# The state update of a linear attention head by head, in two column halves of the TensorE array

## The chip, the cores and the metric

The kernel runs on one core of one Trainium2 chip. The metric is the device time of one execution in microseconds (us), from the first to the last instruction and the little that lies around them. An engine is named as in the profile: PE is TensorE (PEld its weight loads), DVE VectorE, ACT ScalarE, POOL GpSimd, SP the queue that issues most transfers.

## What is computed

A linear attention with a decaying state, then two feed-forward networks on its output. Batch 4, 8 heads, 768 time steps, head size 48:

```python
for t in range(S):
    kt, vt, rt, wt = (k[:, :, t], v[:, :, t], r[:, :, t], w[:, :, t])
    cur = np.einsum('bhd,bhe->bhde', u[None] * kt, vt)
    y[:, :, t] = np.einsum('bhd,bhde->bhe', rt, state + cur)
    state = wt[:, :, :, None] * state + np.einsum('bhd,bhe->bhde', kt, vt)
...
h = x @ w_in
g = h * np.clip(h + 3.0, 0.0, 6.0) / 6.0
x = g @ w_out
...
h = x @ w_in2
solu = h * softmax(h)
out = (layernorm(solu) * g_ln) @ w_out2
```

The change concerns the last line of the time loop: the sum over time of the outer products of k and v, one 48x48 state for each head and batch.

## The kernel before

The sequence is cut into 6 blocks (`g`) of 128 steps. With 4 batches that makes 24 tiles `i = 4 g + b`, each of 8 heads. Five stages handle a tile: `stw` clamps and range-checks w, `st0` transposes w and r to the layout head size x time (PE, into PSUM) and forms running products of w (DVE scans, L484 and L490), `st1` does k, `st2` forms the masked products of r and k (`pa`, L543, `am`, L550 to L554) and the decayed k with time on the partitions (`ktok`, L534), and `st3` makes the state update `kv` (L563) and the output `yt` (L578, L585).

Heads go in pairs: two heads of 48 lie at partitions 0 to 47 and 64 to 111 (`DP = 112`). In `st3`, for tiles of all blocks but the last (20 tiles), `kv` is four matmuls, one for a pair of heads: `ktok` of the pair (112 columns) are the weights, `v` of both heads (96 columns) streams through, both with 128 time steps on the partitions, all in float32. Of the 112x96 result only the two 48x48 blocks on the diagonal are wanted. L604 (DVE, from block 1 on) and L606 (ACT, block 0) take them out of PSUM into the state `s_st`.

`yt` works in column quarters of the array (32 or 16 weight columns at output partition 0, 32, 64 or 96), `pa` in row halves (48 rows at partition 0 or 64).

The feed-forward work is threaded between the attention's stages: for each block 16 slots, each with `ffn_in` (9 matmuls 128x512, L635) and `ffn_out` (9, L655), with ACT L639 and L641, DVE L640 and POOL or DVE L643 between them. At the start the first network's weights are also decoded, chunk by chunk: `raw` (loads L353 to L358) goes through DVE L40, L43, ACT L44, DVE L50, L53, then ACT L60 (`w_h`) and DVE L61 (`w_l`). After block 5 the second network runs (L828 to L858).

The attention's PSUM tiles `wt`, `rt`, `kt`, `ktp`, `pa0`, `pa1`, `kv`, `yt` share one pool of three buffers (`ps_a`, L339, L434). A fourth tile can only be written once the last reader of the first is done.

Every engine runs its instructions in the order in which they stand. For PE, DVE and ACT a scheduler sets that order from what it thinks an instruction costs; the loads on SP and the work on POOL are written out by hand for the first ticks (L739 and what follows) and scheduled after that. So a change of one group's form can move other instructions as well.

Of the kernel before, what the change touches and what calls it, by code (L numbers as in the profile page):

```python
# [267 lines left out]
def fast_path(  # L268
# [15 lines left out]
    B, H, S, D = r.shape  # L284
# [5 lines left out]
    HP = H // 2  # L290
    DP = 112
# [38 lines left out]
        out=causal.bitcast(F32), in_=ones, pattern=[[1, P]], compare_op=ALU.is_gt, fill=0.0, base=0,  # L330
# [102 lines left out]
    def ps_tile(nm):  # L433
        return ps_a.tile([P, 4, P], F32, tag="pa", name=nm)  # L434
# [121 lines left out]
    def st3(i):  # L556
        a = at[i]
        g, b = divmod(i, B)
        if g < NG - 1:
            vv = a["v"].rearrange("p h d -> p (h d)")  # L560
            kv = ps_tile("kv")
            for hp in range(HP):
                nc.tensor.matmul(  # L563
                    out=kv[0:DP, hp, 0:2 * D], lhsT=a["ktok"][:, hp, :], rhs=vv[:, hp * 2 * D:(hp + 1) * 2 * D],
                    start=True, stop=True,
                )
        y = ps_tile("yt")

        def inter(c, first):
            for q in range(4):  # L570
                if c < 2:
                    h = 4 * c + q
                    hp, f = h // 2, D * (h % 2)
                    lhs = a["sp"][0:DP, hp, f:f + 32]
                else:
                    hp = q
                    lhs = a["sr"][0:DP, q, :]
                nc.tensor.matmul(  # L578
                    out=y[32 * q:32 * q + 32, c, :], lhsT=lhs, rhs=a["e"][0:DP, hp, :], start=first, stop=not first,
                    skip_group_check=True,  # L580
                )

        def intra(c, heads, lo, n, first, last):
            for q, h in enumerate(heads):
                nc.tensor.matmul(  # L585
                    out=y[32 * q:32 * q + n, c, :], lhsT=a["v"][:, h, lo:lo + n], rhs=a["am"][h % 2][:, h // 2, :],
                    start=first, stop=last, skip_group_check=True,
                )

        for c in range(2):  # L590
            if g > 0:
                inter(c, True)
            intra(c, range(4 * c, 4 * c + 4), 0, 32, g == 0, True)
        intra(2, range(1, H, 2), 16, 32, True, False)
        intra(2, range(0, H, 2), 32, 16, True, g == 0)
        if g > 0:
            inter(2, False)
        if g < NG - 1:
            for j in range(2):
                o, f = 64 * j, D * j  # L600
                dst = s_st[b][o:o + D, :, f:f + D]
                src = kv[o:o + D, :, f:f + D]
                if g > 0:
                    nc.vector.tensor_tensor(out=dst, in0=src, in1=a["sp"][o:o + D, :, f:f + D], op=ALU.add)  # L604
                else:
                    nc.scalar.activation(out=dst, in_=src, func=ACTF.Copy)  # L606
        at.pop(i)
        if b == 0:
            x_t[g] = (
                xp.tile([P, KD, GT], F32R, tag="xh", name="xh"),  # L610
                xp.tile([P, KD, GT], F32R, tag="xl", name="xl"),
            )
        xh, xl = x_t[g]
        sl = slice(b * C, (b + 1) * C)
        xf = y[:, 0:KD, :]
        nc.scalar.activation(out=xh[:, :, sl], in_=xf, func=ACTF.Copy, accum_out=chk[:, 3 * i + 2:3 * i + 3])
        nc.vector.tensor_tensor(out=xl[:, :, sl], in0=xf, in1=xh[:, :, sl].bitcast(F32), op=ALU.subtract)
# [301 lines left out]
```

## Time and profile before

| | |
|---|---|
| time, median of 3 runs | 795.32 us (794.71 to 795.42) |
| the profiled execution's own time | 796.49 us |
| its span, first to last instruction | 794.8 us |
| mean granted clock of TensorE in it, 1 is 2.4 GHz | 0.978 |
| PE busy | 753.4 us (95%) |
| PEld busy | 634.3 us (80%) |
| DVE busy | 543.2 us (68%) |
| ACT busy | 331.9 us (42%) |
| POOL busy | 272.9 us (34%) |

The profile names an instruction by line, engine, operation and tiles. A matmul row gives weight rows * weight columns and then partitions x streamed columns (`128*112 128x96`). One float32 matmul is two records: L563 has 160 for 80 matmuls. Matmuls are pipelined: the length of one record holds its way through the array, so what a matmul costs a full PE is read from the distance between starts, not from its length.

### The profile page before, as it was taken

What the parts mean: (1) busy time and instruction counts of PE and PEld (TensorE: products, weight loads), DVE (VectorE), ACT (ScalarE), POOL (GpSimd) and SP (SyncE); (2) the same over time, 40 slices, a digit from 0 to 9 for tenths busy, and PEclk for the clock granted to TensorE, in tenths of its full rate; (3) what the DMA queues carried; (4) which work ended last, traced back from release to release, by engine and by line L of the source; (5) the groups of instructions that cost most, each with busy time, mean ns of one, the idle gap of its engine ahead of it and who ended that gap; (6) DMA issues with size and microseconds to landing.
All of it is one profiled execution on the core that took longest, in us unless ns stands there. A gap on an engine that the chain in (4) does not pass through costs nothing. (4 is left out here: it accounts for less than half of the span.)

```text
span 794.8 us, 13227 instructions
## 1 busy us (share of the span) xinstructions
PE 753.4 (95%) x4922; PEld 634.3 (80%) x4922; DVE 543.2 (68%) x1038; ACT 331.9 (42%) x615; POOL 272.9 (34%) x355
## 2 busy tenths in 40 slices
PE   5689898899999999999999999999999999999996
PEld 4567676688888888888888888777889999999996
DVE  5989799856777777777777675895365555555552
ACT  3354544342334433444434334544343443443342
POOL 5487545647333333333232212231122222222210
PEclk9889799999999999999999999999999999999999
DMA  9777455235333433343323212430111111111001
GB/s 167 175 155 162 118 132 138 51 93 124 79 83 91 114 83 84 75 122 81 73 64 93 53 50 61 131 119 1 52 49 40 41 41 51 40 43 48 30 21 35
DMA packets 139432, 64.75 MB, mean 81 GB/s; under 512 B 90848, under 2 KB 133984, under 8 KB 139360
## 3 DMA queue, kind: packets, MB, share of 16 engines
q1 hardware_dynamic: 136768, 59.11, 31.2%
q10 hardware_dynamic: 2592, 4.72, 1.6%
q8 instruction: 41, 0.67, 0.4%
q14 instruction: 31, 0.25, 0.1%
HBM read 54.37 MB, written 9.44 MB: 80 GB/s over the span
## 5 line engine op out<-in xcount | busy, mean ns | idle before, releaser
L639 ACT ACTIVATE t<-h,three 128x512 f32<-128x512 f32 x96 | 65.7, 684 | 176.6 <-PE h L635 175.9
L635 PE MATMUL h<-xh,w_h 128*128 128x512 f32 x288 | 114.4, 398 | 8.7 <-DVE t L640 8.0
L655 PE MATMUL y<-gh,w_h 128*128 128x512 f32 x288 | 117.4, 408 | 0.5 <-ACT ye L661 0.5
L640 DVE SCALAR_TENSOR_TENSOR t<-t,h 128x512 f32<-128x512 f32 x96 | 65.3, 680 | 76.2 <-ACT t L639 75.9
L655 PE MATMUL y<-gl,w_h 128*128 128x512 f32 x288 | 114.0, 396 | 0.3 <-DVE gl L643 0.2
L655 PE MATMUL y<-gh,w_l 128*128 128x512 f32 x288 | 113.6, 394 | 0.0
L635 PE MATMUL h<-xl,w_h 128*128 128x512 f32 x288 | 113.5, 394 | 0.0
L635 PE MATMUL h<-xh,w_l 128*128 128x512 f32 x288 | 113.2, 393 | 0.0
L550 POOL TENSOR_TENSOR am<-ident,d 128x512 f32<-128x512 f32 x48 | 58.5, 1239 | 119.2 <-PE yt L585 119.2
L641 ACT ACTIVATE gh<-t 128x512 fp32r<-128x512 f32 x96 | 60.4, 629 | 55.0 <-DVE t L640 54.6
L643 DVE TENSOR_TENSOR gl<-t,gh 128x512 fp32r<-128x512 f32 x80 | 68.2, 853 | 20.6 <-ACT gh L641 20.4
L635 PEld LDWEIGHTS h<-xh,w_h 128*128 128x128 f32 x288 | 54.7, 190 | 22.9 <-issue 6.8
L67 DVE TENSOR_REDUCE nm<-h 128x1 f32<-128x1024 f32 x24 | 29.4, 1225 | 62.7 <-PE h L828 62.6
L655 PEld LDWEIGHTS y<-gh,w_h 128*128 128x128 f32 x288 | 54.4, 189 | 16.3 <-ACT gh L641 2.1
L855 PE MATMUL po<-w_oh,qh 128*128 128x384 f32 x192 | 67.0, 349 | 0.3 <-ACT qh L844 0.3
L855 PE MATMUL po<-w_oh,ql 128*128 128x384 f32 x192 | 65.2, 339 | 0.1
L855 PE MATMUL po<-w_ol,qh 128*128 128x384 f32 x192 | 65.0, 339 | 0.0
L655 PEld LDWEIGHTS y<-gh,w_l 128*128 128x128 f32 x288 | 54.8, 190 | 11.9
L635 PEld LDWEIGHTS h<-xl,w_h 128*128 128x128 f32 x288 | 54.8, 190 | 11.3
L635 PEld LDWEIGHTS h<-xh,w_l 128*128 128x128 f32 x288 | 54.6, 190 | 11.5
L655 PEld LDWEIGHTS y<-gl,w_h 128*128 128x128 f32 x288 | 54.7, 190 | 11.4 <-DVE gl L643 0.6
L844 ACT ACTIVATE qh<-pt 128x512 fp32r<-128x512 f32 x48 | 26.1, 595 | 79.1 <-PE pt L842 79.1
(118 smaller groups left out, 1518.6 us busy)
## 6 DMA issues: line engine op xcount, KB each, us to landing
raw<-in_moe_w_out_dram SPq DMA_DIRECT2D x24, 384.0 KB
raw<-in_moe_w_in_dram SPq DMA_DIRECT2D x48, 128.0 KB
r<-in_r_dram SPq DMA_DIRECT2D x24, 192.0 KB
k<-in_k_dram SPq DMA_DIRECT2D x24, 192.0 KB
v<-in_v_dram SPq DMA_DIRECT2D x24, 192.0 KB
y1d<-ye ACTq DMA_DIRECT2D x18, 256.0 KB
y<-y1d SPq DMA_DIRECT2D x24, 192.0 KB
out_dram<-os SPq DMA_DIRECT2D x24, 192.0 KB
```

The source lines that it names most:

```text
L67: nc.vector.tensor_reduce(out=nm, in_=h, axis=AX.X, op=ALU.max, negate=True)
L550: nc.gpsimd.tensor_tensor(out=am, in0=ident.unsqueeze(1).to_broadcast([P, HP, C]), in1=dv[:, hh, :].unsqueeze(2).to_broadcast([P, HP, C]), ...
L635: nc.tensor.matmul(out=h, lhsT=a, rhs=b, start=(j == 0), stop=(j == len(ops) - 1))
L639: nc.scalar.activation(out=t, in_=h, func=ACTF.Relu, bias=three)
L640: nc.vector.scalar_tensor_tensor(out=t, in0=t, scalar=6.0, in1=h, op0=ALU.min, op1=ALU.mult)
L641: nc.scalar.activation(out=gh, in_=t, func=ACTF.Copy)
L643: eng.tensor_tensor(out=gl, in0=t, in1=gh.bitcast(F32), op=ALU.subtract)
L655: nc.tensor.matmul(out=y_ps[g][c], lhsT=a, rhs=b, start=(m == 0 and j == 0), stop=(m == M1 - 1 and j == 2))
L844: nc.scalar.activation(out=qh[:, ms, :], in_=pt, func=ACTF.Copy)
L855: nc.tensor.matmul(out=po, lhsT=x[:, m, :], rhs=y[:, m, :], start=(n == 0), stop=(n == 3 * M2 - 1))
```

## The change

Instead of one matmul for a pair of heads there is one for each head. Even heads write output partitions 0 to 47, odd heads 64 to 111, so the two are in the left and the right column half of the array. The weights are 48 columns of `ktok` (not 112), the streamed columns 48 of `v` (not 96). Only wanted blocks are computed. The readers L604 and L606 (numbered the same) now find an odd head's block at columns 0 to 47 of its row in PSUM, where they found it at 48 to 95.

```diff
         if g < NG - 1:
-            vv = a["v"].rearrange("p h d -> p (h d)")
             kv = ps_tile("kv")
-            for hp in range(HP):
+            for h in range(H):
+                o = 64 * (h % 2)
                 nc.tensor.matmul(
-                    out=kv[0:DP, hp, 0:2 * D], lhsT=a["ktok"][:, hp, :], rhs=vv[:, hp * 2 * D:(hp + 1) * 2 * D],
-                    start=True, stop=True,
+                    out=kv[o:o + D, h // 2, 0:D], lhsT=a["ktok"][:, h // 2, o:o + D], rhs=a["v"][:, h, :],
+                    start=True, stop=True, skip_group_check=True,
                 )
...
             for j in range(2):
                 o, f = 64 * j, D * j
                 dst = s_st[b][o:o + D, :, f:f + D]
-                src = kv[o:o + D, :, f:f + D]
+                src = kv[o:o + D, :, 0:D]
```

On PE the group `kv` keeps its place between `ffn_in` and `yt` in every tile. The scheduler also moves some instructions of the first 180 us. Two of these places matter below.

First, the queue of loads on SP where the w and the v of tile 8 are loaded. Before (the second of the two v's, and the w behind the raw block, are tile 8's):

```order
L387 DMA w<-in_w_dram 128x8x48
L394 DMA v<-in_v_dram 128x8x48 x2
L353 DMA raw<-in_moe_w_in_dram 128x1x256 x2
L354 DMA raw<-in_moe_w_in_dram 128x1x256
L358 DMA raw<-in_moe_w_out_dram 128x768
L387 DMA w<-in_w_dram 128x8x48
L387 DMA k<-in_k_dram 128x8x48
```

and now:

```order
L387 DMA w<-in_w_dram 128x8x48
L394 DMA v<-in_v_dram 128x8x48
L387 DMA w<-in_w_dram 128x8x48
L353 DMA raw<-in_moe_w_in_dram 128x1x256 x2
L354 DMA raw<-in_moe_w_in_dram 128x1x256
L358 DMA raw<-in_moe_w_out_dram 128x768
L394 DMA v<-in_v_dram 128x8x48
L387 DMA k<-in_k_dram 128x8x48
```

Tile 8's w and v have changed places around a block of four raw loads. On ACT, at the same point of the program, tile 8's range checks (`junk`) have moved ahead of a `t` and a `dec`:

```order
 L466 ACTIVATE junk,chk<-w,b_hi 128x384
-L639 ACTIVATE t<-h,three 128x512
-L44 ACTIVATE dec<-dec 128x768
-L463 ACTIVATE junk,chk<-w,b_lo 128x384
-L466 ACTIVATE junk,chk<-w,b_hi 128x384
+L463 ACTIVATE junk,chk<-w,b_lo 128x384
+L466 ACTIVATE junk,chk<-w,b_hi 128x384
+L639 ACTIVATE t<-h,three 128x512
+L44 ACTIVATE dec<-dec 128x768
 L60 ACTIVATE w_h<-dec 128x768
```

So `t`, `dec` and `w_h` all stand behind the arrival of that w now; before, only `w_h` did.

Second, DVE after the state update of tile 7, the last one beside the weight decoding:

```order
 L604 TENSOR_TENSOR s_st_121<-kv,sp 48x4x48
 L61 TENSOR_TENSOR w_l<-dec,w_h 128x768
-L640 SCALAR_TENSOR_TENSOR t<-t,h 128x512
 L604 TENSOR_TENSOR s_st_121<-kv,sp 48x4x48
-L484 SCALAR_TENSOR_TENSOR q<-wt,ones 112x128 x3
-L617 TENSOR_TENSOR xl<-yt,xh 128x3x128
-L484 SCALAR_TENSOR_TENSOR q<-wt,ones 112x128
-L488 RECIPROCAL e<-q 112x4
-L539 TENSOR_REDUCE d<-r 128x8
+L640 SCALAR_TENSOR_TENSOR t<-t,h 128x512
+L484 SCALAR_TENSOR_TENSOR q<-wt,ones 112x128
```

The second L604, the last reader of `kv` in PSUM, stands ahead of L640 now.

## Rows read from the trace of the kernel before

**Rows 1.** Stretch: length, busy (count) of PE PEld DVE ACT POOL, PEclk, DMA share, GB/s.
```profile
62.00:157.00 95.00, 80.88 (x589) 64.40 (x588) 87.22 (x136) 43.59 (x75) 54.85 (x55) 0.92 0.49 118
157.00:500.00 343.00, 343.00 (x2523) 282.87 (x2522) 241.67 (x458) 135.86 (x255) 116.05 (x134) 1.00 0.35 84
```
**Rows 2.** Timeline of PE, tile 10's update: start us, us, instruction, count.
```profile
217.93 0.39 PE L635 MATMUL h<-xh,w_l 128*128 128x512 f32 x1
218.16 0.93 PE L563 MATMUL kv<-v,ktok 128*112 128x96 f32 x8
219.02 0.43 PE L578 MATMUL yt<-e,sp 112*32 112x128 f32 x8
...
220.70 0.50 PE L655 MATMUL y<-gh,w_h 128*128 128x512 f32 x1
```
**Rows 3.** Line L563, PE: duration ns min/median/max, first and last start.
```profile
L563 PE MATMUL kv<-v,ktok x160: 243/262/501, 15.9 to 405.3; 128*112 128x96 f32 x160
```
**Rows 4.** Timeline of PE, the row halves of one tile.
```profile
208.75 1.16 PE L543 MATMUL pa<-e,q 48*128 48x128 f32 x16
209.84 0.50 PE L655 MATMUL y<-gh,w_h 128*128 128x512 f32 x1
```
**Rows 5.** Timeline of PE, a tile of the last block, without kv.
```profile
483.47 0.39 PE L635 MATMUL h<-xh,w_l 128*128 128x512 f32 x1
483.78 0.43 PE L578 MATMUL yt<-e,sp 112*32 112x128 f32 x8
```
**Rows 6.** Timeline of PE and DVE around tile 2's update; in brackets the idle time before.
```profile
41.72 1.81 PE L563 MATMUL kv<-v,ktok 128*112 128x96 f32 x8 [0.24 <-DVE am L554]
43.45 1.94 PE L585 MATMUL yt<-am,v 128*32 128x128 f32 x32
...
46.07 0.56 DVE L617 TENSOR_TENSOR xl<-yt,xh 128x384 fp32r<-128x384 f32 x1 [1.89 <-ACT xh L616]
```
**Rows 7.** Timeline of SP, POOL, ACT and DVE around the load of tile 8's w.
```profile
72.99 0.37 SPq L387 DMA_DIRECT2D w<-in_w_dram  x1
...
70.63 0.20 POOL L386 MEMSET w<- 128x128 f32 x1
...
73.24 0.67 ACT L639 ACTIVATE t<-h,three 128x512 f32<-128x512 f32 x1
75.07 0.85 ACT L44 ACTIVATE dec<-dec 128x768 f32<-128x768 f32 x1 [1.16 <-DVE dec L40]
79.45 0.61 ACT L463 ACTIVATE junk<-w,b_lo 128x384 bf16<-128x384 f32 x1 [3.53 <-DMA w<-in_w_dram]
80.80 0.83 ACT L60 ACTIVATE w_h<-dec 128x768 fp32r<-128x768 f32 x1
...
81.66 0.96 DVE L61 TENSOR_TENSOR w_l<-dec,w_h 128x768 fp32r<-128x768 f32 x1 [2.70 <-ACT w_h L60]
```
**Rows 8.** Timeline of DVE after tile 7's update, and the product that PE waits for.
```profile
152.52 0.96 DVE L61 TENSOR_TENSOR w_l<-dec,w_h 128x768 fp32r<-128x768 f32 x1
153.62 0.69 DVE L640 SCALAR_TENSOR_TENSOR t<-t,h 128x512 f32<-128x512 f32 x1
154.34 0.36 DVE L604 TENSOR_TENSOR s_st<-kv,sp 48x192 f32<-48x192 f32 x1
...
162.65 0.68 DVE L518 TENSOR_TENSOR q<-kt,q 112x512 f32<-112x512 f32 x1
```
**Rows 9.** Timeline of PE: idle stretches beside the decoding, and the next transposes.
```profile
140.99 0.47 PE L635 MATMUL h<-xh,w_h 128*128 128x512 f32 x1 [1.22 <-DVE t L640]
154.80 0.62 PE L439 MATMUL rt<-ident,r 128*112 128x128 f32 x4 [1.90 <-issue]
165.55 0.55 PE L532 MATMUL ktp<-ident,q 112*128 112x112 f32 x4
```
**Rows 10.** PE right after two of these: stretch, length, busy (count), PEclk, DMA share, GB/s.
```profile
141.00:144.40 3.40, 3.40 (x28) 1.00 0.00 0
156.20:159.50 3.30, 3.30 (x9) 0.50 0.74 182
```

## The prediction

> **What bounds the kernel now.** I read the busy time by stretch first, then the timeline of PE around the changed line, then the idle stretches of PE and DVE before 160 us. By stretch [rows 1]: from 157 to 500 us PE is busy in every microsecond at the full clock while DVE has 242 us of work in 343, so what a group costs on PE there is time of the kernel. From 62 to 157 us it is DVE that is full (87 of 95 us, it decodes the first network's weights beside its other work), and PE waits for 14 us in sum. The changed line runs from 15.9 to 405.3 [rows 3]. Of the 20 state updates, tiles 8 to 19 lie in the PE-bound stretch, 4 to 7 beside the decoding, 0 to 3 before it.
>
> **What one update costs now.** Take tile 10 [rows 2]. The last `ffn_in` matmul starts at 217.93, the first `kv` record 0.23 later, the first `yt` record at 219.02: 1.09 us from the one to the other. Inside `kv` the 8 records (4 matmuls, two passes each) start at 218.16, and the last of them ends 0.93 later; less its length of 0.262 [rows 3] seven distances fill 0.67 us, 0.096 for a pass of 112 weight columns. From the last start to `yt` it is 0.19, so 0.095 more than a pass: PE runs empty before it goes on in column quarters. `kv` itself uses the whole array like the matmul before it, and pays nothing at its entry.
>
> **What one update costs then.** The two column halves are a new form for the trace; I build them from the nearest rows. Entry: where `yt` follows a full-array matmul with no `kv` between, it is 0.31 from start to start [rows 5] against 0.23 into `kv`; the half form should pay the same, 0.31. The first weights are then no longer loaded behind the matmul before. The row halves show that price: 16 passes in 8 pairs take 1.09 us until the next group [rows 4]; without 0.095 for running empty that is 1.00, or 8 pairs at 0.112 and some 0.10 for the first 128 weight columns. For 48 columns I take 0.04. Pairs: the row halves do run side by side, two passes in 0.112; so do the column quarters, 56 passes in 14 rounds between 219.02 and 220.70 [rows 2], 0.113 a round with the same allowance. Both have 128 columns, `kv` now has 112 and takes 0.096, so the distance goes with the columns, 0.86 to 0.88 ns each; 48 columns make 0.042, and I take 0.045 for a pair. Eight heads in two passes are 8 pairs. Exit: 0.095, as now. Sum: 0.31 + 0.04 + 8 x 0.045 + 0.095 = 0.805 us against 1.09, so 0.285 saved, and 12 x 0.285 = **3.4 us** in the PE-bound stretch. Bounds: with the halves in full accord and no emptying between halves and quarters 0.38 each, 4.6 us; with the pair as slow as the rows that there are (0.096 to 0.113) it is a loss of 0.12 to 0.26 each, 1.5 to 3.1 us. I take the value near the rows scaled by columns, since three rows lie on one line.
>
> The Trainium skill says otherwise of such small matmuls: TensorEngine Tiling (Array Packing), section Instruction Overhead, holds that one with a single streamed column takes as long as one with about 60, and warns not to tile a dimension that is already small. Our 96 columns become 48, below that. No row of this trace has fewer than 96 streamed columns in such a group, so it can't be weighed here; by it a pair would take the time of 60 columns, an estimated 0.053, an update would save 0.22 and the twelve 2.6 us.
>
> The readers L604 and L606 take the same number of elements from another place in PSUM: nothing, DVE and ACT cover them as now.
>
> **The start.** Tile 2's update runs at the half clock: 1.73 us from the first `kv` record to `yt` [rows 6]. Halved speed doubles the terms: 0.08 + 8 x 0.09 + about 0.15 = 0.95, so up to 0.8 sooner for `yt`, `xh` and DVE's `xl`, for which DVE sat idle for 1.89 us. DVE is then nearly full until 157, so this could reach the end of the decoding; loads, which keep their pace, may take it back. Ends 0 and 0.8, I take **0.4**.
>
> **The load of tile 8's w.** At 81.66 DVE waits 2.70 us for `w_h`; ACT had been standing at L463 until 79.45 for the w of tile 8, issued at 72.99 behind a raw block [rows 7]. Now it is issued ahead of that block. It waits there for POOL to fill the tile's padding at 70.63, so it goes out at about 70.9, two microseconds sooner. From issue to L463 it was 6.46 us; I expect L463 at 77.4. But L463 and L466 now stand ahead of `t` (L639) and `dec` (L44) on ACT, so these queue behind the load too. From L463 to `w_h` it was 1.35 us (79.45 to 80.80); with 0.6 for `t` and 0.8 for `dec` (their lengths less the overlap of neighbours) it is 2.75, and `w_h` starts at 80.1, not 80.80: DVE goes on **0.7** sooner, and from there to 157 it has little idle to swallow that [rows 1]. If the load comes as late as before, the same queue costs 1.4: those are the ends. What the w is moved past: the four raw loads go out 1.0 later, for a chunk that DVE takes up after the two in work; and tile 8's v, now behind them, is needed at 175.
>
> **The hand-over from DVE to PE.** At 154.80 PE has been idle for 1.90 us before the transposes `rt` [rows 9]. The profile names no releaser; the three buffers of the attention's PSUM pool do: `kv`, `yt` and `wt` hold them, and `kv` is free when DVE's second L604 ends, 154.34 + 0.36 = 154.70 [rows 8]. That L604 now stands right behind L61, which ends at 153.48; it ends at 153.86, and `rt` starts 0.84 sooner. And there is the clock. After this idle of 1.90 us the granted clock was 0.50, half of 2.4 GHz, for 3.3 us; after one of 1.22 us [rows 9] it stayed at 1.00 [rows 10]. The idle stretch here shrinks to 1.06, so I expect the full clock, which gives back half of the 3.3 us, 1.65. Not all of 2.5 arrives: PE is in front of its next transposes `ktp` at 165.55, and these need DVE's `q`, done at 162.65 + 0.68 = 163.33, whose chain begins with POOL and doesn't move here. PE can gain 165.55 - 163.4 = **2.1**; then `ktp` is what is late next. Ends 0.8 (the clock drops all the same) and 2.1.
>
> **Sum.** 3.4 + 0.4 + 0.7 + 2.1 = 6.6 us, from the profiled execution's 796.49 to 789.9. The median of the runs shown stands 1.2 below that execution: 795.32 - 6.6 = **788.7**.
>
> **Rivals.**
> 1. The pair of small passes has a floor near that of 60 columns. For it: nothing narrower than 96 streamed columns is in the trace. Against: distance and columns are in proportion where there are rows. 2.6 in place of 3.4: 789.5. Chance 0.2; by the page named above this is the case to expect.
> 2. The moves before 160 us don't pay: w lands late behind ACT's new order, or the clock drops all the same. For: ACT's margin is under a microsecond, and the clock rests on two idle stretches. Left are 3.4 and 0.8: 791.1, and with the loss of 1.4 on ACT 792.5. Chance 0.2.
> 3. The halves share a round no better than full passes: a pair takes 0.096 to 0.113, and break-even is (1.09 - 0.445) / 8 = 0.081. A loss of 1.5 to 3.1, less 1.5 from the other moves (0.7 and 0.8): 795.3 to 796.9, no change. Against: the three rows on one line. Chance 0.05.
> 4. The change doesn't do what it says: left and right half run one after the other, 16 passes in series. Place: the same twelve groups. Price: 0.445 + 16 p against 1.09, a loss for the group from p = 0.040 on; with 1.5 gained elsewhere the kernel is slower than before from p = 0.048, and measurably so (1.6 us more, 0.2%, about what a measurement of this kernel can tell) from 0.056. With today's 0.096 it is 0.89 a group, 10.7 us, and 804.5. Against: both row halves and column quarters share their rounds [rows 2, 4]. Chance 0.05.
>
> **How the numbers follow.** The forecast has 0.47, rivals 1 and 2 have 0.2 each, 3 and 4 have 0.05 each, and 0.03 stays for what I don't see, taken as slower too. Faster by over 0.2% (below 793.7) are the forecast and rivals 1 and 2: 0.87. Rival 3 and half of rival 4 are no change: 0.07. Slower: 0.06. The range goes down to 786.5 (the upper bound of 4.6 for the twelve groups and 0.8 at the start give 787.1, and runs differ by some 0.4), and up to 793.0, which takes in rival 2 with the loss on ACT; what lies above is rivals 3 and 4 and the remainder.
>
> **What would show it.** In the trace of the changed kernel: L563 with 320 records of 48 weight and 48 streamed columns, two starts close together every 0.045 us, and 0.8 us from the last `ffn_in` start to `yt` (0.87 by rival 1, above 1.09 by 3 and 4); L463 of tile 8 starting at about 77.4, DVE's wait before L61 below 2 us; idle of about 1.1 before the `rt` near 154 and a clock of 1.00 behind it; PE still busy throughout from 157 to 500. It is wrong if the distance between pairs is above 0.081, if the w lands after 78, or if PE gains waits in the long stretch.

## The result, and the profile after

| | before | changed |
|---|---|---|
| time, median of 6 runs each | 795.07 us (794.06 to 796.63) | 786.95 us (786.0 to 788.9) |
| ratio, with its 95% interval | | 0.9901 (0.9885 to 0.9917) |
| the profiled execution's own time | 796.49 us | 786.0 us |
| mean granted clock in it | 0.978 | 0.985 |

The medians lie 8.1 us apart, 1.0%. The profiled executions lie 10.5 apart, since the one of before stands near the top of its range and the one of the change at the bottom of its own. What of the 10.5 belongs to the change is the matter of the experiments. One execution of 1079.89 us at a granted clock of 0.634, of the kernel with the heads in another order, is left out of that kernel's median below.

The page of the changed kernel, its span and the busy time of each engine:

```profile
span 784.3 us, 13547 instructions
...
PE 746.7 (95%) x5082; PEld 624.8 (80%) x5082; DVE 540.5 (69%) x1038; ACT 331.2 (42%) x615; POOL 271.9 (35%) x355
```

The two stretches of [rows 1], with the columns they have there:

```profile
62.00:157.00 95.00, 83.86 (x647) 66.22 (x646) 87.30 (x140) 45.44 (x79) 61.95 (x60) 0.95 0.52 124
157.00:500.00 343.00, 342.21 (x2633) 278.65 (x2632) 246.73 (x469) 140.23 (x263) 113.32 (x132) 1.00 0.36 87
```

The shape is that of before: DVE full until 157, then PE full and never waiting long. PE has 160 records more and is busy for 6.7 us less in the whole span.

**The update in the long stretch.** The changed line first (it answers to [rows 3]):

```profile
L563 PE MATMUL kv<-v,ktok x320: 208/208/316, 16.0 to 395.3; 128*48 128x48 f32 x160
```

and the timeline of PE for tile 10 [rows 2]:

```profile
210.74 0.39 PE L635 MATMUL h<-xh,w_l 128*128 128x512 f32 x1
211.06 0.56 PE L563 MATMUL kv<-v,ktok 128*48 128x48 f32 x16
211.56 0.43 PE L578 MATMUL yt<-e,sp 112*32 112x128 f32 x8
```

From the last `ffn_in` start to `yt` it is 0.82 here where it was 1.09; by the single records 0.813 against 1.090. The 16 records run from 211.06 to 0.56 later; less the length of one, 0.208, there are 0.35 us between the first start and the last. Record by record that is 0.080 to the second pair and then six times 0.045. `yt` follows 0.14 behind the last start.

**The start**, PE and DVE around tile 2's update [rows 6]:

```profile
42.50 0.88 PE L563 MATMUL kv<-v,ktok 128*48 128x48 f32 x16
43.32 1.12 PE L585 MATMUL yt<-am,v 128*32 128x128 f32 x32
...
45.86 0.56 DVE L617 TENSOR_TENSOR xl<-yt,xh 128x384 fp32r<-128x384 f32 x1 [0.97 <-ACT xh L616]
```

**Tile 8's w**, on SP, ACT and DVE [rows 7]:

```profile
70.25 0.37 SPq L387 DMA_DIRECT2D w<-in_w_dram  x1
...
74.36 0.62 ACT L463 ACTIVATE junk<-w,b_lo 128x384 bf16<-128x384 f32 x1 [1.22 <-DMA w<-in_w_dram]
...
75.71 0.67 ACT L639 ACTIVATE t<-h,three 128x512 f32<-128x512 f32 x1
76.28 0.84 ACT L44 ACTIVATE dec<-dec 128x768 f32<-128x768 f32 x1
77.52 0.84 ACT L60 ACTIVATE w_h<-dec 128x768 fp32r<-128x768 f32 x1 [0.40 <-DVE dec L53]
...
68.29 1.47 DVE L61 TENSOR_TENSOR w_l<-dec,w_h 128x768 fp32r<-128x768 f32 x1
...
78.52 1.16 DVE L61 TENSOR_TENSOR w_l<-dec,w_h 128x768 fp32r<-128x768 f32 x1
```

The w goes out at 70.25 and L463 takes it at 74.36, 4.1 us later, where it had been 6.46. DVE's wait of 2.70 before L61 is gone. The two L61 are the fifth and sixth of the 16 in the program; they are good milestones, because DVE works through the decoding almost without a pause, and their distance is 10.23 here and was 13.00 (68.66 to 81.66).

**The hand-over**, DVE and then PE [rows 8, 9]:

```profile
147.88 0.96 DVE L61 TENSOR_TENSOR w_l<-dec,w_h 128x768 fp32r<-128x768 f32 x1
148.87 0.36 DVE L604 TENSOR_TENSOR s_st<-kv,sp 48x192 f32<-48x192 f32 x1
149.26 0.69 DVE L640 SCALAR_TENSOR_TENSOR t<-t,h 128x512 f32<-128x512 f32 x1
...
149.34 0.62 PE L439 MATMUL rt<-ident,r 128*112 128x128 f32 x4 [1.08 <-issue]
...
158.89 0.60 PE L532 MATMUL ktp<-ident,q 112*128 112x112 f32 x4 [0.27 <-DVE q L518]
```

and the stretch right behind that `rt`, PE's clock in the third column from the right [rows 10]:

```profile
149.50:153.50 4.00, 4.00 (x21) 3.34 (x20) 2.19 (x6) 0.63 (x1) 3.57 (x10) 1.00 0.67 162
```

Idle of 1.08 before `rt`, a clock of 1.00 behind it, and `ktp` waiting for DVE's `q`: all as forecast. The experiments show that this looked better than it was.

### The profile page after: what moved, and what is told of

Read it like the earlier page. It is cut to its first block, busy times and chain, and to the rows that moved or that the text cites. A ratio compares the mean times of both kernels' runs of the same rounds, so it can differ in the third digit from the quotient of the medians.

```text
span 784.3 us, 13547 instructions
## 1 busy us (share of the span) xinstructions
PE 746.7 (95%) x5082; PEld 624.8 (80%) x5082; DVE 540.5 (69%) x1038; ACT 331.2 (42%) x615; POOL 271.9 (35%) x355
## 5 line engine op out<-in xcount | busy, mean ns | idle before, releaser
L635 PE MATMUL h<-xh,w_h 128*128 128x512 f32 x288 | 114.3, 398 | 5.7 <-DVE t L640 5.6
L640 DVE SCALAR_TENSOR_TENSOR t<-t,h 128x512 f32<-128x512 f32 x96 | 65.2, 680 | 73.6 <-ACT t L639 73.4
L635 PE MATMUL h<-xl,w_h 128*128 128x512 f32 x288 | 113.5, 394 | 0.0
L635 PE MATMUL h<-xh,w_l 128*128 128x512 f32 x288 | 113.3, 394 | 0.0
L643 DVE TENSOR_TENSOR gl<-t,gh 128x512 fp32r<-128x512 f32 x80 | 66.7, 834 | 19.3 <-ACT gh L641 19.1
L635 PEld LDWEIGHTS h<-xh,w_h 128*128 128x128 f32 x288 | 54.9, 191 | 19.8 <-issue 4.7
L635 PEld LDWEIGHTS h<-xh,w_l 128*128 128x128 f32 x288 | 54.7, 190 | 11.4
L635 PEld LDWEIGHTS h<-xl,w_h 128*128 128x128 f32 x288 | 54.7, 190 | 11.3
```

The source lines that it names most:

```text
L635: nc.tensor.matmul(out=h, lhsT=a, rhs=b, start=(j == 0), stop=(j == len(ops) - 1))
L640: nc.vector.scalar_tensor_tensor(out=t, in0=t, scalar=6.0, in1=h, op0=ALU.min, op1=ALU.mult)
L643: eng.tensor_tensor(out=gl, in0=t, in1=gh.bitcast(F32), op=ALU.subtract)
```

## The experiments

Each kernel ran beside the kernel before, on the same chip. The edits are shown shortened. Lines that an edit adds shift the line numbers in its rows; tile names say which instruction it is (L474 is L463, L605 and L647 are L604 and L640, and with quarters L643 is L635).

### The loads alone, and the loads put back

```diff
 # before, "wearly": tile 8's v is queued behind the raw block (chunk 7)
+        if i == 8:
+            tc.add_manual_dep(v_load, raws[7], NoSync)
 # changed, "wlate": tile 8's w is queued behind the raw block
+            if i == 8 and nm == "w":
+                tc.add_manual_dep(w_load, raws[7], NoSync)
```

The first has the order of SP and of ACT that the changed kernel has there, the second that of before; nothing else moves on any engine.

> The kernel before, with all its matmuls, and one thing of the change: tile 8's w goes out ahead of the block of four raw loads and its v behind it, and ACT's two range checks of that w stand ahead of t and dec. PE, DVE and POOL keep the order of before. My theory (the order of the loads alone carries the largest early gain): L463 of tile 8 starts at about 74.5 us instead of 79.45, DVE's wait of 2.70 before L61 is gone, tile 5's first kv record starts 3.0 sooner than before (about 92.0 instead of 94.96), tile 8's about 3 to 4 sooner (171.5 to 172.5 instead of 175.44), and the kernel takes 791.2 to 792.1 us against 795.1. The idle time of about 1.9 us before rt near 150 and the half clock behind it stay, since DVE's L640 still stands ahead of L604. Rival (the shorter updates pull the early work forward and the new order of loads only follows): 795.1, no change, with another wait of 2 to 3 us on DVE or PE before 120.

> The changed kernel with the loads put back: tile 8's w behind the block of four raw loads and its v ahead of it, ACT's range checks of it behind t and dec, all other engines as in the changed kernel. My theory: DVE's wait before L61 at about 81 us comes back with 2 to 3 us, tile 5's first kv record starts at about 94.5 instead of 91.54, and the kernel takes 3.0 to 3.9 us more than the changed one, 790.0 to 790.9. The hand-over near 150 keeps its gain (idle before rt about 1.1, clock 1.00 behind it). Rival: 787, as the changed kernel, the load's time being hidden by something else.

ACT and DVE of the kernel before with the w early:

```profile
74.59 0.62 ACT L474 ACTIVATE junk<-w,b_lo 128x384 bf16<-128x384 f32 x1 [0.77 <-DMA w<-in_w_dram]
...
69.76 1.46 DVE L61 TENSOR_TENSOR w_l<-dec,w_h 128x768 fp32r<-128x768 f32 x1
80.19 0.95 DVE L61 TENSOR_TENSOR w_l<-dec,w_h 128x768 fp32r<-128x768 f32 x1
```

and of the changed kernel with the w late:

```profile
79.22 0.61 ACT L474 ACTIVATE junk<-w,b_lo 128x384 bf16<-128x384 f32 x1 [3.48 <-DMA w<-in_w_dram]
...
68.48 1.45 DVE L61 TENSOR_TENSOR w_l<-dec,w_h 128x768 fp32r<-128x768 f32 x1
81.43 0.96 DVE L61 TENSOR_TENSOR w_l<-dec,w_h 128x768 fp32r<-128x768 f32 x1 [2.65 <-ACT w_h L60]
```

From L61 to L61 it is 10.43 with the w early and 12.95 with the w late, whatever the matmuls: the order of the loads, with the order on ACT that goes with it, decides about this wait. It is worth 2.6 and 2.7 us there. Of the twelve profiles that are read here the four with the w late have 6.44 to 6.50 us from its issue to L463, the eight with the w early 2.8 to 4.4. At the end less is seen. The changed kernel with the w late took 789.83 us (788.89 to 790.84), 2.9 more than the changed one's 786.95, and 2.2 more than its 787.61 in a later comparison. But the kernel before with the w early took 793.8 (790.42 to 796.56, 12 runs) beside 794.7, ratio 0.9992 (0.9976 to 1.0008). That was a miss, so it ran once more:

> The kernel before with tile 8's w ahead of the raw block once more, since its first runs spread over 6 us and left the gain open. My theory as the first traces correct it: between the fifth and the sixth L61 on DVE 10.2 to 10.7 us instead of 13.0, of which an execution keeps what its first 70 us don't take away; 2.4 by the median, 792.4. Rival: the gain is given back beside the decoding, and it stays at 0.9 or less, 794 or more.

794.17 us (791.58 to 796.59, 12 runs) beside 795.87, ratio 0.9985 (0.9969 to 1.0001), with 10.45 us from L61 to L61 (70.60 to 81.05). The distance is there both times; the time at the end is 0.6 and 1.2 us shorter by the ratios, with 2.5 at the edge of the second interval. PE's idle before `rt` near 153 was 1.05 in the one profile and 1.89 in the other, with no half clock behind it either time. How much of the 2.6 an average execution keeps stays open, between some 1 us here and 2.2 to 2.9 above.

### The late updates alone, the early ones alone

```diff
-            for h in range(H):
+            for h in range(H) if i >= 8 else ():        # "late12"; "early8": i < 8
 ...
+            else: the four matmuls of before, and their readers
```

> Column halves only in the twelve updates of tiles 8 to 19; tiles 0 to 7 keep the matmuls of before, and with them SP, PE and POOL keep the order of before, while a few ACT and DVE instructions behind 180 us trade places. My theory: 0.278 us from each of the twelve groups (0.81 us from the last ffn_in start to yt instead of 1.09), in sum 3.3: 791.7 us against 795.1, and all stretches before 175 us as before. Rival (PE is not what bounds the long stretch, or the moved DVE work makes PE wait there): less than 1.7, so 793.4 or more. Second rival (each pair has a floor near the time of 60 columns): 2.6, so 792.5, with 0.053 us between pairs.

> Column halves only in the eight updates of tiles 0 to 7, before and beside the weight decoding; tiles 8 to 19 keep the matmuls of before. SP, PE, POOL stand as in the changed kernel. My theory: everything of the change but the twelve times 0.278: the start, tile 8's w, the hand-over, 4.8 us by the medians (8.1 less 3.3) and up to 6.5 by the profiled executions: 790.3, down to 788.6. Rival (the two parts don't add up, because time gained early is lost at a later wait such as the transposes' data): 793 or more.

The late ones alone: 792.93 us (789.5 to 793.77) beside 794.7, ratio 0.9971 (0.9959 to 0.9984), 2.3 us with 1.3 to 3.3. Each group has 0.813, as in the changed kernel, with 0.045 between pairs. Its profiled execution reached the fifth L61 only at 71.33 (68.66 before, with the same instructions up to there), and its tile 8's w, which goes out late, cost it 12.33 from the fifth to the sixth; so the stretch itself is the better measure: from tile 8's first `kv` to the end of the span it is 791.2 - 175.9 = 615.3 us, against 794.8 - 175.4 = 619.4 before. The early ones alone: 790.47 (789.99 to 792.66), ratio 0.9954 (0.9939 to 0.9969), 3.7 us with 2.5 to 4.8, and 618.6 for that last stretch. The two parts were expected at 3.3 and 4.8, which lie at the upper ends of their intervals; 2.3 and 3.7 make 6.0 of the 8.1 (7.9 by the ratio), so some 2 us of the whole are not found in the parts.

### The order of the heads

```diff
-            for h in range(H):
+            for h in (*range(0, H, 2), *range(1, H, 2)):
```

> The changed kernel with the eight heads of an update in another order: the four even heads (left column half) first, then the four odd ones (right half). Same matmuls, same columns, same work on every other engine; only neighbours now lie in the same half. My theory (what pays is that two halves share a round of 0.045 us): 16 passes come one after the other, 0.045 each at least, 0.72 us in place of 0.36, so 1.15 to 1.2 us from the last ffn_in start to yt instead of 0.81, 12 x 0.36 = 4.3 us and half as much again in the early tiles: 791.3 to 793 us against 787 for the changed kernel. Rival (what pays is only that the unwanted blocks are no longer computed, half the columns in and half out): the group keeps 0.81 us and the kernel 787.

792.0 us at the median, ratio 0.9951 (0.9931 to 0.9971): 4.4 more than the changed kernel's 787.61 beside it, 4.0 by the ratios. The rows are from a second profile:

> The kernel with the four even heads ahead of the four odd ones once more, for its rows: it took 4 us more than the changed kernel beside it, but its profiled execution ran at a granted clock of 0.634, and there the first odd passes started beside the last even ones, so the halves seemed to share some of their rounds even in this order. If 12 or 13 rounds are left of 16, a group is 0.18 to 0.22 us longer than the 0.81 of the changed kernel, 2.2 to 2.7 in twelve, and the rest of the 4 lies in the early tiles; if all 16 are in series, 0.36 longer, 1.17.

```profile
232.61 0.39 PE L635 MATMUL h<-xh,w_l 128*128 128x512 f32 x1
232.93 0.78 PE L563 MATMUL kv<-v,ktok 128*48 128x48 f32 x16
233.64 0.43 PE L578 MATMUL yt<-e,sp 112*32 112x128 f32 x8
```

From the last `ffn_in` start to `yt` 1.03 us, between the 0.81 and the 1.15 to 1.2 of the two expectations. Less the 0.208 of a record the group has 0.57 between first and last start. Record by record, the first five starts are 0.080 and then three times 0.045 apart. The sixth follows 0.006 behind the fifth, and from there on two rows of starts run through each other: one goes on from the fifth by 0.045, up to 0.350 from the group's first start; the other goes from the sixth by 0.080 and then by 0.045, up to 0.571. A record does not name its half, but read as the even and the odd heads these are 12 rounds: four even passes alone, four beside the first four odd ones, four odd ones alone. So halves do share a round of 0.045, which is what pays (16 passes in series would need 0.080 and fourteen times 0.045, 0.71), and the first odd pass starts ahead of three even ones that stand before it in the order. Twelve groups times 0.215 are 2.6 us; the rest of the 4.0 to 4.4 was not resolved (an early group at the half clock grows by 0.35). If it were the removal of the unwanted blocks alone that pays, this order, which removes the same ones, would have stayed at 0.81 and 787.

### Quarters in place of halves, in the long stretch

```diff
+            for hp in range(HP) if i >= 8 else ():
+                for lo, n in ((0, 32), (32, 16)):
+                    for par in range(2):
+                        o = 64 * par + lo
+                        matmul(out=kv[o:o + n, hp, 0:D], lhsT=ktok[:, hp, o:o + n], rhs=v[:, 2 * hp + par, :])
```

> The changed kernel, but in tiles 8 to 19 each head's 48 columns go as 32 and 16 in two column quarters of the array, so that kv is in the same form as yt right behind it: 16 matmuls (32 passes) in four quarters, 8 rounds as before. Theory: the running empty between halves and quarters goes, 0.09 to 0.13 us a group, 1.1 to 1.6 in twelve: 0.68 to 0.72 us from the last ffn_in start to yt, and 785.4 to 785.9 against 787. Rival (a round of four instructions has a floor of its own, by the quarters of yt 0.028 us for one instruction): a round takes up to 0.113, a group 0.545 more, 6.5 us in sum, 793.5.

```profile
211.33 0.39 PE L643 MATMUL h<-xh,w_l 128*128 128x512 f32 x1
211.65 0.53 PE L571 MATMUL kv<-v,ktok 128*32 128x48 f32 x32
212.01 0.42 PE L586 MATMUL yt<-e,sp 112*32 112x128 f32 x8
```

0.68 us from `ffn_in` to `yt`, 0.13 less than with halves, twelve times that is 1.6. The time is 785.99 us (785.33 to 786.55), against 787.61 for the changed kernel beside it; ratio to before 0.9885 (0.9861 to 0.9909). Twice the instructions cost nothing that shows. Of the 0.13, 0.10 are the emptying between two forms of the array: `yt` starts 0.036 behind the last start of `kv`, where it was 0.139. The other 0.03 lie in the rounds, 0.328 from first to last start and not 0.356. The Trainium skill, TensorEngine Tiling (Array Packing), section Key Properties, says that changing the tiling mode drains TensorE; the trace agrees, at 0.10 us for halves to quarters. Against the changed kernel the gain at the end is small beside the spread (786.05 to 789.07 there, and the two ratios' intervals overlap), but the stretch shows it: from tile 8's first `kv` to the end it is 613.8 us, where the changed kernel's two profiles have 615.4 and 615.1.

### The second L604 put back behind L640

```diff
+                    if i == 7 and j == 1:
+                        tc.add_manual_dep(l604, l640[14], NoSync)
```

> The changed kernel with DVE's second L604 of tile 7 put back behind L640, as before the change. The scheduler answers with one y matmul ahead of the transposes rt on PE, and a sum d that moves on DVE. By the forecast's term for the hand-over (0.8 to 2.1) it takes 787.8 to 789.0; by what the first runs show (21.3 to 21.4 us from the last L61 to tile 8's kv where the orders are those of before and the clock stays up, 21.0 with the new order) it costs 0.3: 787.3, and the idle of PE ahead of rt says nothing of the time.

```profile
150.72 0.69 DVE L647 SCALAR_TENSOR_TENSOR t<-t,h 128x512 f32<-128x512 f32 x1
151.44 0.36 DVE L605 TENSOR_TENSOR s_st<-kv,sp 48x192 f32<-48x192 f32 x1
...
151.91 0.62 PE L440 MATMUL rt<-ident,r 128*112 128x128 f32 x4 [1.10 <-issue]
...
160.80 0.55 PE L533 MATMUL ktp<-ident,q 112*128 112x112 f32 x4
```

787.43 us (786.26 to 788.49) beside the changed kernel's 787.61: the place of L604 is worth nothing that can be measured. The buffer does release `rt` as the forecast had it (L604 ends at 151.80, `rt` starts at 151.91). But the scheduler has put a `y` matmul ahead of `rt`, which PE then need not do later, and the transposes `ktp` start at 160.80, 2.0 behind the end of `q`, with no wait of PE between `rt` and them; in the changed kernel PE came to `ktp` ahead of `q` and stood for 0.27. From the sixteenth L61 to tile 8's `kv` it is 21.15 us here and 21.02 there.

### Both kernels once more

> The changed kernel once more, for what differs between two executions of it. What belongs to the change should come back: 10.2 us between the fifth and the sixth L61 on DVE (13.0 before), 0.81 us for an update in the long stretch. What was chance should not, or not always: the L40 of 0.58 us at 93.3 on DVE, where five other profiles have 1.63 beside the same gl on POOL, and the place of the half-clock stretches. 787.0, and its profile up to 3 us above the first one's 786.0.

> The kernel before once more, for what differs between two executions of it. If the half clock behind the idle of 1.9 us ahead of rt near 154 belongs to it, it is there again (22.9 us from the last L61 on DVE to tile 8's kv); if it is chance, as the same idle without it in the kernel with halves in tiles 8 to 19 says, it may be 21.3. The 13.0 us from the fifth to the sixth L61 should be there again. 794.8.

787.61 us (786.05 to 789.07), ratio 0.9901 (0.9876 to 0.9926); and 795.5 (794.33 to 797.43) beside 795.87 for the same kernel. The second execution of before at the hand-over, DVE and PE:

```profile
153.59 0.96 DVE L61 TENSOR_TENSOR w_l<-dec,w_h 128x768 fp32r<-128x768 f32 x1
...
155.86 0.62 PE L439 MATMUL rt<-ident,r 128*112 128x128 f32 x4 [1.89 <-issue]
```

and a stretch behind it, where the first execution had the half clock:

```profile
158.00:162.00 4.00, 4.00 (x21) 3.33 (x20) 1.03 (x3) 1.30 (x2) 3.92 (x5) 1.00 0.58 148
```

The idle of 1.89 is there, the half clock behind it is not. Two more profiles with that idle (the late updates alone, and the second one with the w early) have no half clock there either. So of the four profiled executions with this idle it came in one: the first one of before, on which the forecast was built. With the sixteenth L61 as a milestone too, the two kernels' two executions read so (us):

| stretch | before | before, again | changed | changed, again |
|---|---|---|---|---|
| start to the fifth L61 | 68.66 | 69.30 | 68.29 | 69.79 |
| fifth to sixth L61 (tile 8's w) | 13.00 | 13.41 | 10.23 | 10.60 |
| sixth to sixteenth L61 | 70.86 | 70.88 | 69.36 | 70.82 |
| sixteenth L61 to tile 8's `kv` | 22.92 | 21.28 | 21.02 | 21.06 |
| tile 8's `kv` to the end | 619.34 | 619.02 | 615.39 | 615.09 |
| span | 794.8 | 793.9 | 784.3 | 787.4 |

Two rows differ by the change both times: 2.4 to 3.2 in the second, 3.6 to 4.3 in the fifth (of which twelve times 0.277 are 3.3). The 1.9 in the fourth row is 0.2 when repeated. The 1.5 in the third belongs to one of the two executions of the changed kernel.

## Why the prediction was right, and where it was not

The time (786.95 for a forecast of 788.7, range 786.5 to 793.0) and the sign are right, and the sum of 6.6 lies near the 7.2 to 8.1 of the medians. But two of its four terms were mis-sized, by some 1.9 us each and in opposite directions, and that these errors cancel is luck.

**The twelve updates, 3.4: right.** 0.813 measured for a forecast of 0.805, a pair of 0.045 as taken, 0.277 saved a group, 3.3 in sum. The pieces came out too: 0.319 to enter (0.31), 0.035 more than a pair for the first weights (0.04), 0.094 more than a pair to leave (0.095). Scaling the distance of passes with their columns held down to 48. One thing in it was read loosely: the 112 columns of `kv` were its weights (96 stream through), the 128 of the quarters are streamed columns (their weights have 32 or 16). The halves have 48 of both and can't tell which count matters; the quarters of `kv`, with at most 32 weight columns and 48 streamed, take 0.043 a round, so the larger of the two counts fits all these rows. Rival 1 falls. The Trainium skill, TensorEngine Tiling (Array Packing), section Instruction Overhead, gives one streamed column the same latency as 60; taken as a distance of starts that is an estimated 0.053 for a pair, and the trace disagrees, with 0.045. The latency of which the page speaks no run here measures. Rival 2 was right for the hand-over and wrong for the load. Rivals 3 and 4 fall too, though the order of the heads shows what rival 4 stood on: four rounds more cost a group 0.215.

**The start, 0.4: not settled.** The mechanism is as forecast, the group itself went from 1.74 to 0.81 us and DVE's wait from 1.89 to 0.97. But the fifth L61 comes at 68.3 to 69.8 in either kernel, and the difference between two executions of one is larger than the term. All twelve profiles together hint at more than 0.4: the five with the early matmuls of before reach it at 68.7 to 71.3, 69.9 in the mean, the seven with the new ones at 68.0 to 69.8, 68.6 in the mean.

**Tile 8's w, 0.7: mis-sized, 2.4 to 3.2 at the place itself.** The step that failed is "from issue to L463 it was 6.46 us; I expect L463 at 77.4". It took the 6.46 for the load's own duration and moved it along with the issue. But issued ahead of the four raw loads it was used 4.1 us after its issue (2.8 to 4.4 in eight profiles), so part of the 6.46 went with its place behind them. L463 started at 74.36, not 77.4. `t` and `dec` behind it did come 2.5 and 1.2 later on the clock than before, but DVE did not wait for them, and its wait before L61 was gone, not reduced to 2. The bounds of the term (-1.4 to 0.7) did not hold what happened, because both were built on the same 6.46.

**The hand-over, 2.1: mis-sized, 0.1 to 0.3.** The step that failed is the clock: that after the idle of 1.90 "the granted clock was 0.50" and after 1.06 would be 1.00. Both rows were true and the rule made of them was not: the same idle in three other profiles has the full clock behind it. The term was read from one execution's drop and taken off the median of others; the second profile of before, an execution of 795.59 us, has no such drop. What was left, 0.8 from L604, did not count either, as its reversal shows (21.15 us from the sixteenth L61 to `kv`, against 21.02 and 21.06). The forecast of the rows (idle of about 1.1, full clock, `ktp` waiting for `q`) came true and proved little, since the sixteenth L61 to `kv` takes 21.3 in the kernel before, with the idle of 1.89.

So 3.3 + 2.6 + 0.2 make 6.1 of a difference of 7.2 to 8.1. The remainder, 1 to 2 us, was not settled. There are three candidates. The start is one, with the 1.3 between the two means above; the ranges overlap, so it is a hint. The fifth row of the table is another, with 0.3 to 1.0 more than the twelve groups explain. The last is the third row: the DVE order there is the same, but the changed kernel meets one collision of DVE and POOL less often (last section). In five profiles with the early matmuls of before it was met five times, in seven with the new ones four times; that is too few to call it shown.

## What to carry to other kernels

Small matmuls in different column parts of the array pay when neighbours in the order lie in different parts, and more when they have the same form as the group behind them; price them by the distance of starts, scaled with the larger of the weight and the streamed columns, as it held here from 48 to 128. When a load moves ahead of others in a queue, do not carry its time from issue to use along: part of that can be the queue. And a clock drop or the outcome of a collision that one profile shows may be an event of that execution; ask a second profile before a term is built on it.

## What the runs showed that had not been expected

One DVE instruction takes 0.58 or 1.65 us at the same place in the same program. DVE and POOL of the changed kernel, first and second execution, where L40 of the decoding meets `gl`:

```profile
93.18 4.06 POOL L643 TENSOR_TENSOR gl<-t,gh 128x512 fp32r<-128x512 f32 x1 [3.68 <-ACT gh L641]
...
93.30 0.58 DVE L40 TENSOR_SCALAR dec<-raw 128x768 f32<-128x768 f32 x1
```
```profile
94.92 1.36 POOL L643 TENSOR_TENSOR gl<-t,gh 128x512 fp32r<-128x512 f32 x1 [3.67 <-ACT gh L641]
...
95.03 1.67 DVE L40 TENSOR_SCALAR dec<-raw 128x768 f32<-128x768 f32 x1
```

POOL starts 0.11 ahead of DVE in both. Once DVE runs at its usual pace and POOL needs 4.06 us, once POOL needs 1.36 and DVE is held for 1.1. The Trainium skill, SBUF — State Buffer, section Who interferes with whom, says that DVE in certain modes and POOL take turns at a shared pair of ports, and that whichever issues first makes the other one wait. The two outcomes fit that; which engine the records show first does not tell the winner, though, at a distance of 0.11 us. In the twelve profiles DVE kept its pace three times. For DVE, which bounds this stretch, the difference is 1.45 us from one L61 to the next (6.5 or 5.05), of which the next distance gives 0.27 back in these two (9.42 or 9.69). What part it has in the spread of the runs was not measured, and it was not tried to steer it.

The half clock, too, comes at different places in executions of one kernel: behind the idle of 1.9 us before `rt` in one of the two of before.
